# Moving all loads to one queue and fixing the start-up and tail order of an adaLN transformer block

## The chip, the cores and the metric

The kernel runs on one core of a Trainium2 chip (trn2). The metric is the device time of one execution in microseconds (us); where several executions were timed, the median is given with the lowest and highest. The names of the engines are those of the profile: PE does matmuls and transposes, DVE is VectorE, ACT is ScalarE, POOL is GpSimd, SP is SyncE. "PEclk" is the clock granted to PE, as a share of full speed.

## The reference

One transformer block on 2048 tokens of width D = 448. The vector `c` is turned into six modulation vectors. Each of the two halves of the block is a layernorm whose result is scaled and shifted by two of them, and whose output is multiplied by a third.

```python
mod = (silu(c) @ w_mod).reshape(1, 6, 1, -1)
sa, ca, ga, sb, cb, gb = mod[:, 0], mod[:, 1], ...          # cut
h = layernorm(x) * (1 + ca) + sa
x = x + ga * attention(h, wqkv, wo)      # 16 heads of 28, window of 8 tokens at distance 2
h = layernorm(x) * (1 + cb) + sb
x = x + gb * (silu(h @ w1) @ w2)         # hidden width 1792
```

## The kernel before

Tokens are split into even and odd ones, so that a window of 8 at distance 2 becomes 8 neighbours. There are six token groups (k = 0 to 5). The modulation is folded into the weights: `w_pad` is `wqkv` with its rows times `1 + ca`, `bq` is `sa @ wqkv` as a bias, `w1` is scaled by `1 + cb`, `wo` and `w2` by `ga` and `gb`.

The start-up has to produce, in this order of dependence: `scT` (silu of c, turned to a column), `modc_bf` (one modulation vector as columns, sixteen little matmuls into `ps_c`), `onep` (one plus it), twelve pieces of `w_pad`, `ps_b` and `bq`, and four rounds of layernorm on four token tiles each (statistics on DVE, power on POOL, `nmr` on DVE, `xn` on ACT, transpose on PE, copy to `h1T` on DVE). The order of the instructions on each engine is chosen by the framework's scheduler, except where the source adds an `after(later, earlier)`.

```python
# loads: three issuing engines
nc.sync.dma_start(out=x_all[:, 0:4, :], ...)
nc.scalar.dma_start(out=c_row[:], in_=c[0:1, :])
nc.scalar.dma_start(out=wmod_sb[:, 0:3, 0:2 * D], ...)
...                                                     # cut
nc.gpsimd.dma_start(out=wqkv_st[:, 0:3, :], ...)
nc.sync.dma_start(out=x_all[:, 4:8, :], ...)
nc.gpsimd.dma_start(out=wmod_sb[:, 0:3, 2 * D:6 * D], ...)
...                                                     # cut
# zero fills of the weights, all on POOL
nc.gpsimd.memset(wmod_sb[64:128, 3, :], 0.0)
nc.gpsimd.memset(wqkv_st[64:128, 3, :], 0.0)
nc.gpsimd.memset(w_pad[64:128, 3], 0.0)
nc.gpsimd.memset(w_pad[:].rearrange(...)[:, :, DH:32], 0.0)
...                                                     # cut: silu, ps_c, onep
for kt in range(NKT):
    for typ in range(3):
        nc.vector.tensor_scalar(out=w_pad[...], in0=wqkv_st[...], scalar1=onep[...], op0=ALU.mult)
...                                                     # cut: ps_b, bq
for q4 in range(1, 4):                                  # layernorm of groups of four tiles 1 to 3
    v_, a_ = layernorm_T([4 * q4 + i for i in range(4)], h1T, e_of_u, "a", use_pe=True)
    after(v_[0], bq_ins, "startup: critical vector-engine work first")
    ...
# the main loop
for k in range(NGRP + 1):
    if k < NGRP:
        attn_S(k, qkv_cur); pes = [attn_phase1(k, g, qkv_cur) for g in range(NG)]
    if k >= 1:
        post_a(UT_OF_GROUP[k - 1])      # ps_o, layernorm, DMA transposes into h2T
    if k < NGRP:
        attn_V(k, qkv_cur)
        for g in range(NG): attn_phase2(k, g, pes[g])
    if k + 1 < NGRP:
        qkv_next = project(k + 1)       # ps_p, evicted by ACT as "qkv"
    if k >= 1:
        post_b(prev, hid)               # ps_h, silu on ACT
        post_c(prev, hid)               # ps_y, output
```

## Time and profile before

| kernel before | us |
|---|---|
| time, 4 runs | 273.92 (272.8 to 274.78) |
| time of all its runs when the changed kernel was measured, those 4 included, 16 runs | 274.71 (272.8 to 276.0) |
| span of the profiled execution | 272.7 |
| first "qkv" eviction (end of start-up) | 57.51 |
| last group (from 237.2) | 35.5 |

The first lines of the profile's page for the kernel before: the busy time and share of each engine, then PE's busy tenths and its granted clock in 40 equal slices of the span (6.8 us each), and the load rate.

```profile
PE 206.4 (76%) x1902; PEld 130.8 (48%) x1902; DVE 154.3 (57%) x366; ACT 165.8 (61%) x292; POOL 33.1 (12%) x56
...
PE   0035635979799299988999889998994399914993
...
PEclk9999999999999779999999999999999579995999
...
GB/s 248 346 346 357 35 0 0 4 0 2 0 2 1 38 2 19 17 40 20 2 35 17 42 19 2 34 20 38 2 17 19 59 0 2 34 33 41 0 19 34
```

No engine is full. PE does nothing in the first two slices, is busy about half of the time or less in most of the next five, and is nearly empty again in the two slices "14" near the end (238.6 to 252.2 us). The next fence is the timeline of DVE in the start-up of the kernel before (start, busy time, engine, line, operation, and in brackets how long the engine sat idle before it and what ended the wait).

```profile
14.75 1.68 DVE L148 BATCH_NORM_STATS2 statsa<-x_all 128x6 f32<-128x448 bf16 x3 [7.50 <-DMA x_all<-in_A_x_dram]
16.35 0.14 DVE L154 SCALAR_TENSOR_TENSOR nmra<-mva,rstda 128x4 f32<-128x4 f32 x1
...
21.56 0.17 DVE L214 TENSOR_SCALAR onep_bf<-modc_bf 128x4 bf16<-128x4 bf16 x1
...
22.47 3.04 DVE L222 TENSOR_SCALAR w_pad<-wqkv_st,onep 128x448 bf16<-128x448 bf16 x12
...
31.09 0.17 DVE L238 COPY bq<-ps_q 128x12 f32<-128x12 f32 x1 [0.98 <-PE ps_q L237]
```

DVE takes its instructions in the order that it was given. The scheduler put statistics of the second x block ahead of the first `nmr`, and so DVE sat 7.5 us on a load, until 14.75, with nothing else done. `bq` comes at 31.09; three rounds of `nmr` follow at 33.9, 40.0 and 45.7 us, in lines left out here. The third view is PE's timeline in the last stretch of the kernel before.

```profile
217.35 11.30 PE L401 MATMUL ps_h<-h2T,w_sb 128*128 128x384 bf16 x56 [1.65 <-DMA h2T<-xn]
228.49 2.81 PE L410 MATMUL ps_y<-w_sb,hid 128*128 128x448 bf16 x14
...
239.65 0.35 PE L391 MATMUL ps_o<-x_all,ident 128*128 128x448 bf16 x1
248.93 10.88 PE L401 MATMUL ps_h<-h2T,w_sb 128*128 128x384 bf16 x56 [8.93 <-DMA h2T<-xn]
259.64 2.81 PE L410 MATMUL ps_y<-w_sb,hid 128*128 128x448 bf16 x14
```

The second half of the block for the last group cannot start until its layernorm and its DMA transposes are through: PE idles 8.9 us ahead of the last `ps_h`, with three short `ps_o` before that.

### The profile page before, as it was taken

The page shows a single profiled execution, that of the slowest core. Times are in us where ns is not written, and L with a number is a line of the kernel's source. Part 1 is how long each engine was busy: PE and PEld are TensorE (multiplying, and loading weights), DVE is VectorE, ACT ScalarE, POOL GpSimd, SP SyncE. Part 2 cuts the span into 40 slices and gives each one's busy share as a digit, 9 for nine tenths or more (in the row PEclk, how much of TensorE's full clock was granted, in tenths as well). Part 3 has the DMA queues.
Part 4 walks back from the last instruction along what each step waited for, and adds up shares of the span by engine and source line. Part 5 has one row for each costly group of instructions (what it writes and reads, how often), then busy time and mean ns, then how long its engine had stood idle before and what let it go on. Part 6 is the DMA issues. An engine that isn't in the chain of part 4 may idle for free.

```text
span 272.7 us, 4747 instructions
## 1 busy us (share of the span) xinstructions
PE 206.4 (76%) x1902; PEld 130.8 (48%) x1902; DVE 154.3 (57%) x366; ACT 165.8 (61%) x292; POOL 33.1 (12%) x56
## 2 busy tenths in 40 slices
PE   0035635979799299988999889998994399914993
PEld 0025623546466185655556555566852255502651
DVE  4056384579999995989209892099968500040000
ACT  2054076698768573899718996289944666241830
POOL 4890111000000000010010100101011000210001
PEclk9999999999999779999999999999999579995999
DMA  7999100000000100031010200001000200012000
GB/s 248 346 346 357 35 0 0 4 0 2 0 2 1 38 2 19 17 40 20 2 35 17 42 19 2 34 20 38 2 17 19 59 0 2 34 33 41 0 19 34
DMA packets 15392, 13.30 MB, mean 49 GB/s; under 512 B 9225, under 2 KB 13962, under 8 KB 15370
## 3 DMA queue, kind: packets, MB, share of 16 engines
q1 hardware_dynamic: 11296, 5.54, 8.1%
q0 software_dynamic: 1280, 4.65, 4.8%
q10 hardware_dynamic: 2794, 2.81, 3.4%
q8 instruction: 15, 0.25, 0.4%
q14 instruction: 7, 0.06, 0.1%
HBM read 9.06 MB, written 1.84 MB: 40 GB/s over the span
## 4 chain that ended last, share of the span: by engine, by line
PE 43%; DVE 25%; issue 13%; DMA 8%; ACT 6%; POOL 3%; SPq 0%; POOLq 0%; ACTq 0%
PE ps_h L401 15%; PE ps_y L410 13%; DMA x_all<-in_A_x_dram 5%; DVE mx L347 4%; DVE xm L349 3%; PE ps_p L324 3%; DMA h2T<-xn 3%; PE pst L165 2%; PE O L378 2%; DVE rs L369 2%; DVE statsb L148 2%; DVE statsa L148 2%; DVE pn L372 2%; ACT w_sb L261 2%; DVE S L336 2%
## 5 line engine op out<-in xcount | busy, mean ns | idle before, releaser
L401 PE MATMUL ps_h<-h2T,w_sb 128*128 128x384 bf16 (+1 forms) x336 | 56.7, 329 | 18.3 <-DMA h2T<-xn 17.5
L403 ACT ACTIVATE hid<-ps_h,b 128x384 bf16<-128x384 f32 (+1 forms) x84 | 44.3, 548 | 16.0 <-PE ps_h L401 13.0
L401 PEld LDWEIGHTS <-w_sb 128*128 128x128 bf16 x336 | 33.8, 103 | 38.1 <-issue 23.8
L324 PE MATMUL ps_p<-h1T,w_pad 128*128 128x344 bf16 (+1 forms) x288 | 47.7, 313 | 1.8 <-ACT qkv L326 1.7
L410 PE MATMUL ps_y<-w_sb,hid 128*128 128x448 bf16 x224 | 45.0, 352 | 0.0
L326 ACT ACTIVATE qkv<-ps_p,bq 128x344 bf16<-128x344 f32 (+1 forms) x72 | 35.6, 562 | 3.3 <-PE ps_p L324 3.0
L324 PEld LDWEIGHTS <-w_pad 128*128 128x128 bf16 x288 | 27.8, 98 | 17.7 <-issue 3.7
L410 PEld LDWEIGHTS <-hid 128*128 128x128 bf16 x224 | 21.9, 98 | 19.9
L347 DVE TENSOR_REDUCE mx<-L 128x14 f32<-128x448 f32 (+1 forms) x24 | 14.0, 621 | 28.2 <-PE L L345 28.2
L414 ACT CAST ot<-ps_y 128x448 bf16<-128x448 f32 x16 | 8.5, 532 | 34.9 <-PE ps_y L412 34.9
L159 ACT ACTIVATE xn<-x_all,nmra,rstda 128x448 bf16<-128x448 bf16 x16 | 10.8, 748 | 26.5 <-DVE nmra L154 24.3
L165 PE MATMUL pst<-ident,xn 128*128 128x128 bf16 x64 | 9.4, 309 | 22.8 <-ACT xn L159 21.7
L415 POOL DMA_DIRECT2D out_dram<-ot x16 | 9.0, 561 | 139.6 <-ACT ot L414 139.6
L148 DVE BATCH_NORM_STATS2 statsb<-x_all 128x6 f32<-128x448 bf16 x16 | 9.5, 610 | 23.8 <-ACT x_all L392 23.6
L378 PE MATMUL O<-pT,V 128*128 128x32 bf16 x344 | 12.6, 179 | 10.4 <-DVE pT L375 10.4
L165 PEld LDWEIGHTS <-xn 128*128 128x128 bf16 x64 | 6.0, 135 | 29.7 <-ACT xn L159 28.6
L378 PEld LDWEIGHTS <-V 128*128 128x128 bf16 x344 | 11.8, 98 | 13.3 <-issue 9.5
L336 DVE COPY S<-qkv 32x1792 bf16<-32x1792 bf16 (+1 forms) x24 | 14.9, 622 | 1.6 <-ACT qkv L326 1.3
L148 DVE BATCH_NORM_STATS2 statsa<-x_all 128x6 f32<-128x448 bf16 x16 | 9.4, 611 | 10.6 <-DMA x_all<-in_A_x_dram 10.6
L363 DVE COPY V<-vs 32x1792 bf16<-32x1792 bf16 (+1 forms) x24 | 15.1, 628 | 0.6
L390 PE MATMUL ps_o<-wo_pad,oT 128*128 128x448 bf16 x64 | 15.4, 352 | 0.0
L369 DVE TENSOR_REDUCE rs<-pe 128x14 f32<-128x448 f32 (+1 forms) x24 | 14.1, 602 | 1.2 <-ACT pe L352 1.1
(89 smaller groups left out, 264.6 us busy)
## 6 DMA issues: line engine op xcount, KB each, us to landing
x_all<-in_A_x_dram SPq DMA_DIRECT2D x4, 448.0 KB, 11.6
out_dram<-ot POOLq DMA_DIRECT2D x16, 112.0 KB, 2.0
w_sb<-in_B_w_dram ACTq DMA_DIRECT2D x1, 1568.0 KB, 25.5
wmod_sb<-in_w_mod_dram POOLq DMA_DIRECT2D x1, 1344.0 KB, 13.4
w_sb<-in_B_w_dram SPq DMA_DIRECT2D x1, 1344.0 KB
wqkv_st<-in_A_wqkv_dram POOLq DMA_DIRECT2D x1, 1008.0 KB, 9.3
wmod_sb<-in_w_mod_dram ACTq DMA_DIRECT2D x1, 672.0 KB
wo_pad<-in_A_wo_dram ACTq DMA_DIRECT2D x4, 98.0 KB
```

What stands on the lines that cost most here:

```text
L148: vops.append(nc.vector.bn_stats(out=stats[:, j, :], in_=x_all[:, U, :]))
L165: nc.tensor.transpose(pst[:, kt, :], xn[:, 128 * kt:128 * kt + 128], ident[:])
L324: nc.tensor.matmul(ps[:, 0:wd], lhsT=w_pad[:, kt, typ, g, :], rhs=h1T[:, kt, e0:e0 + wd], start=(kt == 0), stop=(kt == NKT - 1))
L326: nc.scalar.activation(out=tiles[typ][:, g, 0:wd], in_=ps[:, 0:wd], func=ACTF.Identity, bias=bq[:, typ * 4 + g:typ * 4 + g + 1])
L336: nc.vector.tensor_copy(out=_ap4(S4[:, 0, 0, :], 32 * hq, 32 * hq, ((TMAX * 128, NG), (128, T), (1, BW))), in_=_ap4(qg[:, 0, :], 32 * hq, ...
L347: nc.vector.tensor_reduce(out=mx[:, 0:T], in_=L[:, 0:T, :], axis=AX.X, op=ALU.max)
L369: nc.vector.tensor_reduce(out=rs[:, 0:T], in_=pe[:, 0:T, :], axis=AX.X, op=ALU.add)
L378: nc.tensor.matmul(O[:, j, :], lhsT=V4[:, g, j, :], rhs=pT[:, j, :], start=True, stop=True)
L390: nc.tensor.matmul(ps[:, 0:D], lhsT=oT[:, g, n0:n0 + 128], rhs=wo_pad[:, g, :], start=(g == 0), stop=False)
L401: nc.tensor.matmul(ps[:, 0:n], lhsT=w1_sb[:, kt, f * 128:(f + 1) * 128], rhs=h2T[:, kt, c0:c0 + n], start=(kt == 0), stop=(kt == NKT - 1))
L403: ins = nc.scalar.activation(out=hid[:, f, 0:n], in_=ps[:, 0:n], func=ACTF.Silu, bias=b1[:, f:f + 1])
L410: nc.tensor.matmul(ps[:, 0:D], lhsT=hid[:, f, j * 128:(j + 1) * 128], rhs=w2_sb[:, f, :], start=(f == 0), stop=False)
```

## The change

Its intent is to shorten the start-up and the tail. It has three parts. First, all loads go to the sync engine's queue, in order of need. Second, the instructions of the start-up are chained, so that each engine issues them in program order: the modulation matmuls come ahead of the first transposes, four of the twelve `w_pad` pieces go to ACT, and the statistics of the second x block come behind `bq` and the masks. Third, `post_a` of the last group moves from the round after the last to the end of the last round, ahead of `post_b` of the group before it. Along with the second part, the zero fill of `wo_pad` moves from POOL to DVE, and the fills of two small constants from DVE to POOL.

```diff
-    nc.scalar.dma_start(out=c_row[:], in_=c[0:1, :])
-    nc.scalar.dma_start(out=wmod_sb[:, 0:3, 0:2 * D], ...)
+    nc.sync.dma_start(out=c_row[:], in_=c[0:1, :])
+    nc.sync.dma_start(out=wmod_sb[:, 0:3, 0:2 * D], ...)
...                        # cut: all other loads likewise; wo, w1 and w2 follow at once
+    chains = {"v": [], "a": [], "p": []}
+    def V(ins):            # A, P and G (POOL) alike
+        chains["v"].append(ins)
+        return ins
...
+    mv0, rstd0 = ln_stats([0, 1, 2, 3], "a", wrap=V, wg=G)
+    A(nc.scalar.activation(out=sc_row[:, 0:D], in_=c_row[:], func=ACTF.Silu))
...                        # cut: scT, nmr0
+    G(nc.gpsimd.memset(wmod_sb[64:128, 3, :], 0.0))
+    mod_cols(1, 1, V, P)
+    make_onep(0, 1, V)
+    ev0 = ln_apply([0, 1, 2, 3], mv0, rstd0, h1T, e_of_u, "a", use_pe=True, ...)
...
+    G(nc.gpsimd.memset(wqkv_st[64:128, 3, :], 0.0))
+    G(nc.gpsimd.memset(w_pad[64:128, 3], 0.0))
+    G(nc.gpsimd.memset(w_pad[:].rearrange(...)[:, :, DH:32], 0.0))
...
+            if typ == 2:
+                A(nc.scalar.activation(out=o_, in_=i_, func=ACTF.Identity, scale=onep[0:rn, 0, kt:kt + 1]))
+            else:
+                V(nc.vector.tensor_scalar(out=o_, in0=i_, scalar1=onep[0:rn, 0, kt:kt + 1], ...))
+    mod_cols(0, 0, V, P)
...                        # cut: ps_b, b_unp, bq, masks
+    mv1, rstd1 = ln_stats([4, 5, 6, 7], "a", wrap=V)
+    ev1 = ln_apply([4, 5, 6, 7], mv1, rstd1, h1T, e_of_u, "a", use_pe=True, wv=V, wa=A)
...
+    w1_zero = nc.gpsimd.memset(w1_sb[64:128, 3, :], 0.0)
+    for name in ("v", "a", "p", "g"):
+        for x0, x1 in zip(chains[name], chains[name][1:]):
+            after(x1, x0, "start-up issue order")
...
-        if k >= 1:
+        if 1 <= k < NGRP:
             post_a(UT_OF_GROUP[k - 1])
...
+        if last:
+            post_a(UT_OF_GROUP[k])
         if k + 1 < NGRP:
             qkv_next = project(k + 1)
```

## The prediction

> **What bounds it now.** No engine is full (page, part 1: PE 76%, ACT 61%, DVE 57% of 272.7 us). The timeline has three stretches. (a) 0 to 57.6 us, start-up: a serial chain; PE is busy 25 of 57.6 us. (b) 57.6 to 237.2: PE busy 159 of 180 us. (c) 237.2 to 272.7, the last token group: PE does 2.8 us of ps_o, then waits for layernorm and DMA transposes. ps_h resumes at 248.9 (idle of 8.9 us, released by DMA h2T).
>
> **What the change does.**
> 1. All loads go to the sync queue, in order of need. Bytes are unchanged (9.06 MB read, about 350 GB/s while loading). The Trainium skill, "DMA: Bandwidth & Descriptors", section "Issuing engines are not separate DMA queues", says all issuers share the same 16 engines, so I expect no bandwidth lost or won. An estimate at 346 GB/s: c and the first w_mod columns by about 7 us, w_qkv by 10, everything by 29. None of these should be what waits longest. In before the second x block landed at 14.7 us, and the in-order DVE sat 7.5 us on it, which delayed the first nmr from about 8.5 to 16.4.
> 2. Chained order. The modulation matmuls go ahead of the first transposes, v's part of w_pad goes to ACT (DVE 12 to 8 pieces, 3.04 to 2.0 us), group-1 statistics come after bq. My sum: rstd 7.1, pow 1.04, POOL memset of w_mod 2.33 to about 10.7 (the new gate), ps_c 0.8, onep 12.2, four h1T copies to 13.8, w_pad to 15.8, ps_b 4.3, then 1.4 to bq: about 22 us against 31.26. Part is given back: masks, then three layernorm rounds run nearly serially (statistics 2.4, pow 1.0, four xn 2.7, transpose and copy 1). Before overlapped them more (nmr at 33.9, 40.0, 45.7); I expect 27.3, 35.8, 41.0. Then as before ps_b1 and the w1 scaling (6.83) stand on ACT ahead of the first qkv eviction. First qkv at about 52.5 against 57.5: gain about 5 us.
> 3. post_a of the last group moves ahead of post_b of group 4. Its layernorm and transposes then run under 20 us of PE work, so the 11.8 us between ps_y and ps_h go. Paid back: three ps_o hold three of four PSUM buffers, and ACT's order becomes x_all copies, table load, one hid, three xn (2.06, after nmr), thirteen hid. I expect PE to stall about 2.5 us early in ps_h of group 4 and post_c(4) to start 4 us later than 228.5. Net about 7.7 us.
>
> Stretch (b) keeps its instruction order, so it only shifts.
>
> **Sum.** 273.9 - 5 - 7.7 = about 261 us; 257.5 to 264.5 eight times in ten. Faster by over 2%: 0.96; within 2%: 0.03; slower: 0.01.
>
> **What would show it.** bq copy at 21 to 24 us; first qkv at 51 to 54; DVE not waiting for x at 7 to 15 us; load rate still about 350 GB/s; no PE gap over 2 us between the last ps_y of group 4 and the last ps_h; a new ACT-caused PE stall of 2 to 4 us in ps_h of group 4.
>
> **What would make it wrong.** One queue feeding the engines more slowly, so that w_mod lands after 11 us or w1 after 44; POOL set-up delaying eps or the memsets; DVE and POOL slowing each other at 11 to 17 us; layernorm rounds more or less serial than I summed (2 us either way); the group-5 x_all copies stalling ps_h longer than 4 us.

## The result

| | before | changed |
|---|---|---|
| time, median (lowest to highest) | 274.71 (272.8 to 276.0), 16 runs | 264.66 (263.58 to 266.15), 11 runs |
| ratio | | 0.9637 [0.9608, 0.9667] |
| span of the profiled execution | 272.7 | 262.2 |
| `bq` on DVE | 31.09 | 24.49 |
| `nmr` of the three later rounds | 33.90, 39.95, 45.73 | 30.31, 38.43, 43.77 |
| first qkv eviction | 57.51 | 55.55 |
| start of the S copies of the last group | 190.53 | 189.64 |
| `ps_h` of group 4 starts | 217.35 | 216.47 |
| from there to the end | 55.35 | 45.73 |

A ratio in this document is the mean time of one kernel's fast runs over the mean of the other's fast runs of the same rounds, so it is not quite the ratio of the medians that stand beside it. The brackets hold the 95% interval.

The change made the kernel faster by 3.6%, but it missed the predicted 261.0 us by 3.7 us and came to lie just above the range of 257.5 to 264.5. The page of the changed kernel has the same lines:

```profile
PE 207.6 (79%) x1902; PEld 130.9 (50%) x1902; DVE 157.2 (60%) x361; ACT 167.2 (64%) x296; POOL 28.7 (11%) x53
...
PE   0337425989889479998999969999899657799993
...
PEclk9999999999979959999999999999999959799999
...
GB/s 228 356 328 294 180 0 0 4 0 2 0 0 2 21 23 0 38 0 63 0 2 54 2 60 0 2 35 21 41 2 18 20 60 0 61 2 51 2 20 35
```

The end of the start-up is ACT's first "qkv" eviction, here first in the kernel before, then in the changed one:

```profile
57.51 4.48 ACT L326 ACTIVATE qkv<-ps_p,bq 128x368 bf16<-128x368 f32 x9
```

```profile
55.55 6.35 ACT L370 ACTIVATE qkv<-ps_p,bq 128x368 bf16<-128x368 f32 x12
```

In the page, the slices are now 6.6 us. The end of PE's row has no empty slice any more ("99657799993" where before "4399914993" stood). The start is only a little fuller. There is a new weak place in the clock row, the 7 three places ahead of the first 5 (72 to 79 us). The load rate of the first slices is about as before (228, 356, 328 and 294 against 248, 346, 346 and 357), and a rest is carried in the fifth slice.

DVE in the start-up of the changed kernel:

```profile
12.31 1.46 DVE L245 TENSOR_SCALAR onep_bf<-modc_bf 128x4 bf16<-128x4 bf16 x1
...
15.31 3.61 DVE L272 TENSOR_SCALAR w_pad<-wqkv_st,onep 128x448 bf16<-128x448 bf16 x8
...
24.49 0.17 DVE L285 COPY bq<-ps_q 128x12 f32<-128x12 f32 x1 [0.69 <-PE ps_q L284]
```

The 7.5 us wait for x is gone, as predicted. Two things were not expected. The little `onep_bf` on 128x4 elements took 1.46 us, where the kernel before needed 0.17. And eight pieces of `w_pad` took 3.61 us, where twelve had taken 3.04. What POOL did at that time is in its own timeline:

```profile
11.21 1.21 POOL L260 MEMSET wqkv_st<- 64x1344 bf16 x1
12.37 1.37 POOL L261 MEMSET w_pad<- 64x1536 bf16 x1
...
16.21 1.60 POOL L307 MEMSET w_sb<- 64x1792 bf16 x1
```

POOL's memset of `w_pad` ran from 12.37 to 13.74, and the 1.46 us of `onep_bf` end at 13.77. One of the eight `w_pad` pieces took 1.74 us where the median is 0.33: it started at 16.21, the next one at 17.87, and POOL's memset of `w_sb` ran from 16.21 to 17.81. Copies from PSUM on DVE at the same time (four `h1T` copies, 1.52 us in all) were not lengthened. The Trainium skill has this in "SBUF — State Buffer", section "Who interferes with whom": DVE and POOL share one pair of ports, a copy, cast or `tensor_scalar` in a 2-port mode takes it for the whole instruction, as does a POOL instruction, and the one that comes second "fully blocks". The numbers fit that, and they fit with no sharing: the DVE instructions ended with the memsets. Which of the two came second is not clear from the starts: `onep_bf` started 0.06 us ahead of the memset that it ended with, while the memset before that one (11.21 to 12.42) still ran.

The third place is the end. PE's timeline of the last stretch of the changed kernel:

```profile
216.47 0.90 PE L445 MATMUL ps_h<-h2T,w_sb 128*128 128x384 bf16 x3 [0.60 <-DMA h2T<-xn]
...
221.13 0.81 PE L445 MATMUL ps_h<-h2T,w_sb 128*128 128x384 bf16 x4 [0.52 <-ACT hid L447]
224.38 7.40 PE L445 MATMUL ps_h<-h2T,w_sb 128*128 128x384 bf16 x36 [2.44 <-ACT hid L447]
231.62 2.81 PE L454 MATMUL ps_y<-w_sb,hid 128*128 128x448 bf16 x14
...
240.14 9.26 PE L445 MATMUL ps_h<-h2T,w_sb 128*128 128x384 bf16 x56
249.24 2.81 PE L454 MATMUL ps_y<-w_sb,hid 128*128 128x448 bf16 x14
```

The last `ps_h` follows straight on the last `ps_y` of group 4, at 240.14. What was paid for it is seen in the idle times of 0.52 and 2.44 us behind "ACT hid". And the last fifty-six `ps_h` take 249.24 - 240.14 = 9.10 us from start to start of the next group, where before they took 259.64 - 248.93 = 10.71.

The account of the profiled executions is then: start-up -2.0 us (57.51 to 55.55), the middle +1.1 (the lead at `ps_h` of group 4 is only 217.35 - 216.47 = 0.9), the tail -9.6 (55.35 to 45.73). The sum is -10.5, which is 272.7 less 262.2. The prediction had -5, 0 and -7.7.

Three questions follow. Was the tail's gain really that large, and apart from the rest? Why did the start-up give 2 us and not 5? And where did 1.1 us go in the middle, where no instruction was moved? (One caution on the 2 us: in another execution with the same start-up as the kernel before, the tail run below, the second x block let go 0.7 us sooner and the first qkv came at 56.80; in two more with the changed start-up it came at 55.33 and 55.44. The gain of the start-up is thus 1.3 to 2.2 us, by the pair of profiles.)

### The profile page after: what moved, and what is told of

Read it like the earlier page. It is cut to its first block, busy times and chain, and to the rows that moved or that the text cites. A ratio compares the mean times of both kernels' runs of the same rounds, so it can differ in the third digit from the quotient of the medians.

```text
span 262.2 us, 4748 instructions
## 1 busy us (share of the span) xinstructions
PE 207.6 (79%) x1902; PEld 130.9 (50%) x1902; DVE 157.2 (60%) x361; ACT 167.2 (64%) x296; POOL 28.7 (11%) x53
## 3 DMA queue, kind: packets, MB, share of 16 engines
q0 software_dynamic: 768, 1.84, 2.0%
HBM read 9.06 MB, written 1.84 MB: 42 GB/s over the span
## 4 chain that ended last, share of the span: by engine, by line
PE 35%; DVE 26%; issue 18%; ACT 10%; POOL 4%; DMA 4%; POOLq 0%; SPq 0%; ACTq 0%; DVEq 0%
PE ps_h L445 12%; PE ps_y L454 10%; DVE mx L391 4%; DVE xm L393 3%; DMA h2T<-xn 3%; DVE statsb L180 3%; ACT xn L202 3%; PE ps_p L368 3%; DVE rs L413 2%; ACT qkv L370 2%; PE pst L208 2%; ACT w_sb L333 2%; PE O L422 2%; DVE S L380 2%; PE ps_b L278 2%
## 5 line engine op out<-in xcount | busy, mean ns | idle before, releaser
L445 PE MATMUL ps_h<-h2T,w_sb 128*128 128x384 bf16 (+1 forms) x336 | 54.8, 321 | 10.9 <-DMA h2T<-xn 6.8
L368 PE MATMUL ps_p<-h1T,w_pad 128*128 128x344 bf16 (+1 forms) x288 | 49.0, 319 | 1.3 <-ACT qkv L370 1.2
L447 ACT ACTIVATE hid<-ps_h,b 128x384 bf16<-128x384 f32 (+1 forms) x84 | 43.7, 548 | 7.2 <-PE ps_h L445 4.3
L445 PEld LDWEIGHTS <-w_sb 128*128 128x128 bf16 x336 | 33.0, 101 | 29.3 <-issue 14.2
L434 PE MATMUL ps_o<-wo_pad,oT 128*128 128x448 bf16 x64 | 17.6, 387 | 0.6 <-ACT oT L424 0.6
L419 DVE STREAM_TRANSPOSE pT<-pn 128x448 bf16<-128x448 bf16 (+1 forms) x24 | 14.6, 634 | 0.1
L416 DVE TENSOR_TENSOR pn<-pe,rs 128x448 bf16<-128x448 f32 (+1 forms) x24 | 14.3, 624 | 0.1
L405 DVE STREAM_TRANSPOSE vs<-qkv 128x448 bf16<-128x448 bf16 (+1 forms) x24 | 14.2, 631 | 0.2
```

Of the source, the lines that this page charges most:

```text
L368: nc.tensor.matmul(ps[:, 0:wd], lhsT=w_pad[:, kt, typ, g, :], rhs=h1T[:, kt, e0:e0 + wd], start=(kt == 0), stop=(kt == NKT - 1))
L434: nc.tensor.matmul(ps[:, 0:D], lhsT=oT[:, g, n0:n0 + 128], rhs=wo_pad[:, g, :], start=(g == 0), stop=False)
L445: nc.tensor.matmul(ps[:, 0:n], lhsT=w1_sb[:, kt, f * 128:(f + 1) * 128], rhs=h2T[:, kt, c0:c0 + n], start=(kt == 0), stop=(kt == NKT - 1))
L447: ins = nc.scalar.activation(out=hid[:, f, 0:n], in_=ps[:, 0:n], func=ACTF.Silu, bias=b1[:, f:f + 1])
```

## The experiments

Each run was timed against the kernel before in the same rounds on the same chip. The medians of before in the three lots of runs were 275.29, 274.8 and 274.8 us (11 runs each). In the second lot (the first test of the old queues, the queue move alone, and the two kernels under "Putting it together") one run of before came in at 270.96. Runs over 1.5% above the fastest count as slow and stay out of the ratios, so this one run shuts out five of the other ten; it widens the intervals of the second lot and raises its ratios by about 0.3%, and the record's verdict for all four kernels of the lot is "unclear".

### The tail alone, and the start-up alone

The first theory is that the two parts add: the tail is worth some 9.5 us and the start-up some 2. The rival is that the tail is worth what was predicted and the start-up carries more than its 2 us. The first kernel is before, with the third part of the change alone.

```diff
@@ on the kernel before
-        if k >= 1:
+        if 1 <= k < NGRP:
             post_a(UT_OF_GROUP[k - 1])
...
+        if last:                     # k == NGRP - 1
+            post_a(UT_OF_GROUP[k])
```

> The kernel before with part 3 alone (post_a of the last group ahead of post_b of group 4). Theory A (read from the two traces: tail worth 9.6 us of the 10.5, because the 11.8 us gap goes, about 4 us are paid back in ps_h of group 4, and the last ps_h also runs about 1.6 us faster since PE no longer restarts at a low granted clock after an idle of 9 us): about 9.5 us faster than before, ratio 0.965. My recorded sum: 7.7 us, ratio 0.972. The last ps_h should take about 9.2 us in theory A against 10.9 before.

Measured: 265.03 us (264.12 to 266.58), ratio 0.9643 [0.9596, 0.9691]. The last `ps_h` took 9.1 us from 240.41.

The second kernel is the changed one with the tail put back.

```diff
@@ on the changed kernel
-        if 1 <= k < NGRP:
+        if k >= 1:
             post_a(UT_OF_GROUP[k - 1])
...
-        if last:
-            post_a(UT_OF_GROUP[k])
```

> The changed kernel with the last post_a back at its old place: start-up rework and queue move alone. Theory A: 1 to 2 us faster than before (first qkv at 55.5 against 57.5), ratio 0.993 to 0.997; the last ps_h again takes about 10.7 us at a granted clock under 1. Recorded sum: 5 us faster, ratio 0.982.

Measured: 272.95 us (271.91 to 273.62), ratio 0.9917 [0.9866, 0.9968]; first qkv at 55.33; the last `ps_h` takes 10.7 us again. The tail is worth about 10 us on its own and the start-up about 2. With the old start-up and with the new one, the last `ps_h` is fast if and only if the gap ahead of it is gone: 9.1 us after no wait, 10.7 after the 9 us idle. The granted clock over the last `ps_h` is 0.84 in the kernel before (0.50 in its first 2 us, 1.00 from 253.0 on) and 0.85 with the start-up alone; it is 1.00 in the changed kernel and with the tail alone. The Trainium skill says in "TensorE: Matmul & The Clock Gate", section "What's actually happening", that the clock is halved after an idle window of about 3.4 us and given back after a busy one of that length; the slower restart agrees with it.

Added up, the two medians would give 275.29 - 10.3 - 2.3 = 262.7 us for both parts, 2 us less than the changed kernel took. The intervals are about 1.3 us wide to each side, so this alone shows nothing, but it is on the side of something lost in the middle; "The middle" below settles most of it.

### POOL's zero fills out of the way of DVE

The theory is that POOL's memsets held DVE in the start-up. Here the memsets of `w_pad` and `w1` move ahead of POOL's first power, to 1.6 to 6.1 us, when DVE clears tiles, waits for x and then runs statistics.

```diff
@@ on the changed kernel
+    G(nc.gpsimd.memset(w_pad[64:128, 3], 0.0))
+    G(nc.gpsimd.memset(w_pad[:].rearrange(...)[:, :, DH:32], 0.0))
+    G(nc.gpsimd.memset(w1_sb[64:128, 3, :], 0.0))
     mv0, rstd0 = ln_stats([0, 1, 2, 3], "a", wrap=V, wg=G)
...
-    G(nc.gpsimd.memset(w_pad[64:128, 3], 0.0))
-    G(nc.gpsimd.memset(w_pad[:].rearrange(...)[:, :, DH:32], 0.0))
...
-    w1_zero = nc.gpsimd.memset(w1_sb[64:128, 3, :], 0.0)
```

> The changed kernel with three POOL memsets (two on w_pad, one on w1) moved into POOL's idle time before its first pow (2.7 to 7.8 us). Theory A (DVE's SBUF-to-SBUF bf16 instructions wait for a running POOL memset: onep_bf took 1.46 us and one w_pad piece 1.74 us in after, against 0.15 and 0.33): both fall to their usual time, bq at about 21.7 us instead of 24.5, first qkv at about 52.7 instead of 55.6, total about 2.8 us under the changed kernel, ratio to before about 0.953. Rival (those two instructions are long for another reason, such as waiting for a weight load to land): unchanged, bq at 24.5, ratio 0.963.

Measured: 261.79 us (260.26 to 262.76), ratio 0.9515 [0.9464, 0.9566]. DVE in this run:

```profile
12.28 0.17 DVE L248 TENSOR_SCALAR onep_bf<-modc_bf 128x4 bf16<-128x4 bf16 x1
...
14.19 2.04 DVE L273 TENSOR_SCALAR w_pad<-wqkv_st,onep 128x448 bf16<-128x448 bf16 x8
...
21.81 0.17 DVE L286 COPY bq<-ps_q 128x12 f32<-128x12 f32 x1 [0.69 <-PE ps_q L285]
```

`onep_bf` is back to 0.17 us, the eight pieces to 2.04, and `bq` comes 2.7 us sooner. The later rounds of `nmr` are at 27.62, 35.74 and 41.08, the first qkv at 52.87. The prediction had 27.3, 35.8, 41.0 and 52.5. So with this one collision taken out, the start-up is what the prediction had summed.

An earlier memset could also help in another way, say because `w_pad` is ready sooner. So the next kernel keeps the early memsets and adds three of the same sizes at the old place, onto a scratch tile that nothing reads.

```diff
@@ on the kernel of the last experiment
     G(nc.gpsimd.memset(wqkv_st[64:128, 3, :], 0.0))
+    scratch = const.tile([128, 2688], BF16, name="scratch")
+    G(nc.gpsimd.memset(scratch[64:128, 0:1536], 0.0))
+    G(nc.gpsimd.memset(scratch[:, 0:2688].rearrange("p (x d) -> p x d", d=14)[:, :, 0:4], 0.0))
+    G(nc.gpsimd.memset(scratch[64:128, 0:1792], 0.0))
```

> e3 plus three POOL memsets of the same sizes as those moved, on a scratch tile that nothing reads, at the place the moved ones had. Theory A: the two long DVE instructions come back, bq at 24 to 24.5 us, ratio to before about 0.963 again. Rival (moving helped because w_pad and w1 were ready earlier, a matter of data and not of POOL being busy): as fast as e3, 0.953.

Measured: 263.98 us (262.92 to 265.14), ratio 0.9603 [0.9554, 0.9651]; first qkv at 55.51. First DVE, then POOL in this run:

```profile
12.22 1.45 DVE L248 TENSOR_SCALAR onep_bf<-modc_bf 128x4 bf16<-128x4 bf16 x1
...
15.22 3.65 DVE L277 TENSOR_SCALAR w_pad<-wqkv_st,onep 128x448 bf16<-128x448 bf16 x8
...
24.43 0.17 DVE L290 COPY bq<-ps_q 128x12 f32<-128x12 f32 x1 [0.69 <-PE ps_q L289]
```

```profile
12.27 1.37 POOL L265 MEMSET scratch<- 64x1536 bf16 x1
...
16.64 1.60 POOL L267 MEMSET scratch<- 64x1792 bf16 x1
```

The stalls are back to within 0.04 us, though no instruction reads what these memsets write. A dependence is excluded. The six times (262.92 to 265.14 us) and the six of the run before (260.26 to 262.76) do not overlap. So 2.6 of the 3 us that the start-up fell short were DVE held while POOL filled; that the shared port is the reason is the page's account, which no run here tests apart.

### The queues apart from the order

The prediction gave the queue move no worth in bandwidth. The first test puts the loads of the changed kernel back on the old queues, in the old order, with the wo and w2 issues on ACT.

```diff
@@ on the changed kernel
-    nc.sync.dma_start(out=c_row[:], in_=c[0:1, :])
+    nc.scalar.dma_start(out=c_row[:], in_=c[0:1, :])
...                        # likewise all loads, as in the kernel before
-        nc.sync.dma_start(out=wo_pad[32 * hq:32 * hq + DH, :, :], in_=wo_v[hq])
+        nc.scalar.dma_start(out=wo_pad[32 * hq:32 * hq + DH, :, :], in_=wo_v[hq])
```

> The changed kernel with the loads issued as before (c, w_mod head, wo and w2 from ACT, w_qkv and the rest of w_mod from POOL, x and w1 from sync); order of the engines as changed. My reading: in the changed order no instruction waits for the later loads (group-1 statistics start at 25.8 us, x block 2 landed long before), so the queue move is worth little here: within 1 us of the changed kernel, ratio to before 0.960 to 0.968. Rival (the queue move is the gain of the start-up): first qkv back at 57 us or later, ratio about 0.971.

Measured: 269.64 us (266.27 to 271.52), ratio 0.9828 [0.9739, 0.9916], unclear as a verdict, and 5 us worse than expected. ACT's timeline in this run ("ACTq" is the issue of a DMA):

```profile
2.35 12.38 ACTq L131 DMA_DIRECT2D wo_pad<-in_A_wo_dram  x4
...
15.22 1.28 ACT L224 ACT_TABLE_LOAD   x1 [15.22 <-DMA wo_pad<-in_A_wo_dram]
16.51 0.57 ACT L224 ACTIVATE sc_row<-c_row 1x448 bf16<-1x448 bf16 x1
```

The expectation missed because the test was badly built. The four wo issues stood ahead of silu on ACT; from the first to the last of them ACT did nothing else, from 2.35 to 14.73. Each took 0.3 to 0.6 us; the time lies between them, as the third started at 8.17 and the fourth at 14.41. In the compiled program each of the last three, and the w2 issue, waits for a semaphore of an earlier load; the traces show the gaps and not what was waited for. So silu ran at 16.51 where the changed kernel has it near 4.1, `bq` came at 29.08 and the first qkv at 60.14. The loads themselves were not slow. The test was mended later: the same queues, but the wo and w2 issues stand on ACT behind its `w_pad` pieces.

```diff
@@ on the kernel of the last experiment
-    for hq in range(4):
-        nc.scalar.dma_start(out=wo_pad[...], in_=wo_v[hq])       # ahead of everything
-    nc.scalar.dma_start(out=w2_sb[:], ...)
...
+    for hq in range(4):
+        A(nc.scalar.dma_start(out=wo_pad[...], in_=wo_v[hq]))    # behind w_pad
+    A(nc.scalar.dma_start(out=w2_sb[:], ...))
     mod_cols(0, 0, V, P)
```

> The full change with all loads on the old queues again, but this time the four wo issues and the w2 issue stand on ACT behind the last piece of w_pad, so that ACT has nothing to wait for ahead of silu. Theory (the queue itself carries no time; the 5 us of the first old-queue run came from ACT held at 2.4 to 14.8 us by a DMA issue that waits): silu starts at about 4 us as in the full change, bq at 22 to 26 us, first qkv eviction within 2 us of 55.6, time within 2 us of 264.7, ratio to before .957 to .970. Rival (the old queues themselves bring the loads later): first qkv still at 59 us or later, time 268 to 271.

Measured: 265.13 us (264.33 to 266.53), ratio 0.9664 [0.9621, 0.9707]; silu at 3.63, `bq` at 24.62, first qkv at 55.70. ACT in this run:

```profile
3.63 0.57 ACT L221 ACTIVATE sc_row<-c_row 1x448 bf16<-1x448 bf16 x1
```

This is the changed kernel's time within half a us. In the chained kernel the queue is therefore worth nothing in itself that these runs could tell from noise. The Trainium skill, in "DMA: Bandwidth & Descriptors", section "Issuing engines are not separate DMA queues", says the same of the transfers; it adds that issuing from several engines only saves sequencer time, "which is usually small relative to the DMA itself". The time of an issue on ACT is indeed small here (0.3 to 0.9 us each in the two tests). But issues that have to wait, on an engine with work behind them, were not small: 12.4 us of ACT in the first of the two tests.

The next kernel is before, with the queue move alone.

```diff
@@ on the kernel before
-    nc.scalar.dma_start(out=c_row[:], in_=c[0:1, :])
+    nc.sync.dma_start(out=c_row[:], in_=c[0:1, :])
...                        # likewise all loads, in the order of the changed kernel
```

> The kernel before with the queue move alone. In before DVE waited 7.5 us for x block 2 ahead of the first nmr, which came at 16.4 us. My reading: with x block 2 later in one queue the scheduler now puts the first nmr ahead of that wait, so nmr at 8.5 to 9.5, bq some 5 us earlier than 31.3; the later chain keeps part of it: first qkv 2 to 5 us earlier than 57.5, ratio 0.982 to 0.993. Rival (queue choice changes nothing, all issuers share the same engines): ratio 1.000 within 0.004.

Measured: 268.97 us (267.9 to 270.74), ratio 0.9844 [0.978, 0.9907]. The ratio was within what was expected (just below it, 0.981, if the runs of before that the rule shuts out are kept), but the first qkv came at 50.08, 7.4 us sooner than before and 5.5 us sooner than in the fully changed kernel. The rounds of `nmr` in this run:

```profile
8.28 0.17 DVE L154 SCALAR_TENSOR_TENSOR nmra<-mva,rstda 128x4 f32<-128x4 f32 x1 [1.15 <-POOL rstda L152]
...
25.49 0.16 DVE L154 SCALAR_TENSOR_TENSOR nmra<-mva,rstda 128x4 f32<-128x4 f32 x1 [0.68 <-POOL rstda L152]
...
30.60 0.16 DVE L154 SCALAR_TENSOR_TENSOR nmra<-mva,rstda 128x4 f32<-128x4 f32 x1 [0.85 <-POOL rstda L152]
...
36.43 0.16 DVE L154 SCALAR_TENSOR_TENSOR nmra<-mva,rstda 128x4 f32<-128x4 f32 x1 [0.90 <-POOL rstda L152]
```

With the loads on one queue the scheduler no longer puts statistics of x block 2 ahead of the first `nmr`, which comes at 8.28 instead of 16.35. And it keeps running the statistics of later rounds in the holes of earlier ones, so the rounds are about 5 to 6 us apart; in the chained kernel the second and third are 8.1 us apart. POOL's fills (12.38 to 17.91) stretch DVE here too: the twelve `w_pad` pieces take 4.56 us instead of 3.04. Still `bq` comes at 21.66, so this is not what sets the two orders apart. Of the 7.4 us, 3 were lost again on the way in the profiled execution, at 270.32 us one of the slower of the six: the granted clock of the whole run is 0.936 against 0.956 of before, and its row has more weak slices in the first half. All six runs are low (0.936 to 0.949, against 0.95 to 0.956 of before in the same rounds).

So the chained order would be a loss at the first qkv. To see whether this holds at the end, the next kernel has the queue move and the tail, and not the chained order.

```diff
@@ on the kernel of the last experiment
-        if k >= 1:
+        if 1 <= k < NGRP:
             post_a(UT_OF_GROUP[k - 1])
...
+        if last:                     # k == NGRP - 1
+            post_a(UT_OF_GROUP[k])
```

> Before with the queue move and the moved post_a of the last group, without the chained issue order and without the split of w_pad to ACT. Theory (the chained order costs about 5 us against what the scheduler does once the x wait is gone): first qkv eviction at about 50 us instead of 55.6, tail about 9.5 us shorter than before, time 258 to 262, ratio .940 to .955, so faster than the full change. Rival (the first qkv time of the queue-only run does not carry to the end, its time is eaten by the granted clock or by waits in the attention): time 263 to 267, no faster than the full change.

Measured: 259.82 us (256.95 to 261.1), ratio 0.9428 [0.9374, 0.9481]; first qkv at 49.97. It is 4.8 us faster than the full change (timed in other rounds; against before, 0.9428 and 0.9637), with less of it. Then which part of the chained order costs this? The rounds point to the statistics of the second x block, which the chain holds until `bq` and the masks are through. One more kernel moves only these ahead of the copy of `b_unp`, into 4.6 us in which DVE idles for `ps_b`.

```diff
@@ on the changed kernel
+    mv1, rstd1 = ln_stats([4, 5, 6, 7], "a", wrap=V, wg=G)
+    nmr1 = ln_nmr([4, 5, 6, 7], mv1, rstd1, "a", V)
     b_unp = small.tile([128, 12], F32, name="b_unp")
...
-    mv1, rstd1 = ln_stats([4, 5, 6, 7], "a", wrap=V)
-    ev1 = ln_apply([4, 5, 6, 7], mv1, rstd1, ..., wv=V, wa=A)
+    ev1 = ln_apply([4, 5, 6, 7], mv1, rstd1, ..., wv=V, wa=A, nmr=nmr1)
```

> The full change with one thing moved: the statistics, power and nmr of token group 1 stand ahead of the copy of b_unp in DVE's chain, where DVE idles 4.6 us on ps_b, instead of behind bq and the masks. Theory (the chained order makes the layernorm rounds serial behind bq, and that is what the start-up lost against the queue move alone): bq unchanged at 24 to 25 us, nmr rounds at about 24, 33 and 39 us instead of 30.3, 38.4, 43.8, first qkv at 50 to 52 us, time 260 to 262. Rival (other things gate the first qkv: the w1 load and scaling, or the clock): first qkv within 1 us of 55.6, time within 1 us of 264.7.

Measured: 257.57 us (255.81 to 259.58), ratio 0.9388 [0.9341, 0.9435]. This is lower than expected. DVE in this run:

```profile
15.27 2.19 DVE L272 TENSOR_SCALAR w_pad<-wqkv_st,onep 128x448 bf16<-128x448 bf16 x8
...
22.00 0.16 DVE L190 SCALAR_TENSOR_TENSOR nmra<-mva,rstda 128x4 f32<-128x4 f32 x1 [1.20 <-POOL rstda L184]
...
23.04 0.17 DVE L287 COPY bq<-ps_q 128x12 f32<-128x12 f32 x1 [0.69 <-PE ps_q L286]
...
37.27 0.16 DVE L190 SCALAR_TENSOR_TENSOR nmra<-mva,rstda 128x4 f32<-128x4 f32 x1 [1.05 <-POOL rstda L184]
```

All later rounds come 6.5 us or more sooner, and the first qkv at 49.06, 6.5 us sooner than in the changed kernel. `bq` was expected unchanged and came 1.45 us sooner. This was a side effect: the power of this round now stands in POOL's chain ahead of the `w1` memset, which therefore starts at 22.03 instead of 16.21 and no longer meets the `w_pad` pieces, which take 2.19 us instead of 3.61. So, by subtraction, 5.0 of the 6.5 us belong to the order of the statistics and 1.5 to the fill; the two were not run apart.

### The middle

The last question is the 1.1 us that the changed kernel lost between 57 and 203 us. There PE does the same work in the same order in both kernels. The lead at the S copies is 1.97 us twice and then 0.58; the loss falls between the second and the third group. In the profile of the changed kernel the granted clock is 0.50 from 73.8 to 77.0 us. The changed kernel was profiled once more, unaltered.

```diff
@@ on the changed kernel
(no edit)
```

> The full change unaltered, profiled a second time, to see whether the dip of the granted clock to 0.50 at 73.8 to 77.0 us, which took about 1.4 us of the lead of the start-up, belongs to the kernel. Theory (the dip comes with the stretch of work of this kernel and its alignment): a dip in the same slice again, and the S copy of the last group at 202 to 203 us. Rival (the dip falls differently from execution to execution): no dip near 75 us, and the last S copies start about 2 us ahead of before (201.3 us), span about 261.

Measured: 262.65 us, one run (its state is unknown, since one run alone cannot be placed), beside 274.88 of before; span 260.8. (The expectation's 201 to 203 us are not S copies but work some 13 us behind them; the last group's S copies are at 190.53 in before, 189.64 in the changed kernel and 188.35 here.) The two executions of one and the same kernel, with busy times and PEclk of two stretches (the columns are the stretch, its length, busy us and instructions of PE, PEld, DVE, ACT and POOL, the clock, and the share and rate of DMA). First the changed kernel, then its second profile:

```profile
70.20:73.60 3.40, 1.52 (x27) 1.04 (x26) 3.40 (x9) 1.58 (x5) 0.00 (x0) 1.00 0.00 0
73.80:77.00 3.20, 3.20 (x18) 1.53 (x15) 3.20 (x9) 0.69 (x3) 0.00 (x0) 0.50 0.00 0
```

```profile
70.20:73.60 3.40, 1.52 (x32) 1.08 (x30) 3.40 (x8) 1.58 (x4) 0.00 (x0) 1.00 0.00 0
73.80:77.00 3.20, 3.09 (x27) 1.76 (x25) 3.20 (x9) 1.65 (x5) 0.00 (x0) 1.00 0.00 0
```

In both, PE was busy 1.52 of 3.4 us ahead of the place. In the one the clock was then halved for 3 us, in the other it was not. With no dip, the lead of the S copies of the second run is 2.08 us for three groups and 2.18 at the last, so the whole lead of the start-up arrives. The middle's loss in the first profile is the clock's, and not one of order or of waits. The Trainium skill, "TensorE: Matmul & The Clock Gate", section "What's actually happening", calls the window free-running and its effect run-variable; this pair of runs agrees, with 1.4 us between them.

It is not pure chance either, it seems. The time from the S copies of the second group to those of the third is 19.44 us without the dip and 20.8 to 21.0 with it. In five profiles the first qkv falls between 55.3 and 55.7 us, and four of them have the dip (changed, start-up alone, scratch memsets, old queues mended). Of eight others with the first qkv elsewhere one has it there (queue move alone), and one more loses about 2.6 us one group earlier (queue move with tail, 22.1 us from the first to the second S copies against 19.5 in before). Why it should depend on the time of the start stays open: one profile of each kernel is too few.

The timed runs have no trace, but the record gives the mean clock of each. It comes in steps, and the times follow it. The changed kernel has 0.966 in one of twelve runs (263.58 us, the fastest), 0.961 in four (263.95 to 264.1), 0.959 in five (264.03 to 265.27) and 0.955 in two (265.9 and 266.15). The second profile, without the dip, had 0.966, and the first, with it, 0.959. So eleven of twelve runs lost more clock than the one without the dip, though a mean does not say where.

This also bears on the 2 us that were missing when the parts were added. The mean time of before at 0.956 was 273.7 us, and of the start-up alone at the same clock 272.2; the tail alone took 264.5 in its three runs at 0.966. Added up at these clocks the parts give 263.0. The changed kernel took 263.58 and 262.65 us at 0.966. One step lower (0.95 with the old tail, 0.959 with the new one) the sum is 263.9 and the changed kernel 264.8. At equal clock, then, the shortfall is under 1 us. The tail alone simply met the higher clock in three of six runs, the changed kernel in one of twelve.

### Putting it together

The two last kernels try to use what was found. The first bundles several edits of the start-up: the `wmod` and `wqkv` fills (and the masks') early on POOL, the other fills on ACT, the rest of `w_mod` loaded ahead of x blocks 3 and 4, the second modulation vector ahead of the transposes, and the statistics of the second x block ahead of `b_unp`.

```diff
@@ on the changed kernel
+    G(nc.gpsimd.memset(wmod_sb[64:128, 3, :], 0.0))      # ahead of the first power
+    G(nc.gpsimd.memset(wqkv_st[64:128, 3, :], 0.0))
...
     A(nc.scalar.activation(out=sc_row[:, 0:D], in_=c_row[:], func=ACTF.Silu))
+    A(nc.scalar.memzero(w_pad[64:128, 3]))
+    A(nc.scalar.memzero(w_pad[:].rearrange(...)[:, :, DH:32]))
+    A(nc.scalar.memzero(w1_sb[64:128, 3, :]))
...
     make_onep(0, 1, V)
+    mod_cols(0, 0, V, P)
...
+    mv1, rstd1 = ln_stats([4, 5, 6, 7], "a", wrap=V, wg=G)
+    nmr1 = ln_nmr([4, 5, 6, 7], mv1, rstd1, "a", V)
     b_unp = small.tile([128, 12], F32, name="b_unp")
```

> The changed kernel with e3 taken further: the POOL memsets that gate ps_c run before POOL's first pow, three zero fills go to idle ACT, group-1 statistics go into DVE's 4.6 us wait for ps_b. Sum of durations: ps_c at 7.8 instead of 11.3, bq at about 18, nmr of group 1 at about 18 instead of 30.3; then two more serial layernorm rounds of about 8 and 5.5 us as before and the w1 scaling: first qkv at about 43 against 55.6, total about 252 us, ratio about 0.92. If the layernorm rounds are limited by something else than DVE's order, first qkv later than 48.

Measured: 253.95 us (253.13 to 255.81), ratio 0.9292 [0.9234, 0.9349]; `bq` at 20.2, first qkv at 45.6, each some 2 us later than expected. The share of each edit was not measured, except for what the run with the early statistics shows.

The last kernel also takes work out of the start-up that the first group does not need: `project(0)` follows right on `bq`, and the layernorm of later tiles, the scaling of `w1`, `wo` and `w2` go into the attention of the first groups.

```diff
@@ on the kernel of the last experiment
-    late_setup_compute()                 # ahead of project(0)
...
+    ln1_apply()                          # behind project(0)
     for k in range(NGRP + 1):
...
+            if k == 0:
+                qkv_1 = project(1)
+                w1_setup()
...
+        if k == 0:
+            scale_rows(wo_pad[:], g_bc[0], NG)
+            ln_late(2)
+            qkv_next = qkv_1
...
+        if k == 2:
+            ln_late(3)
```

> e7 with project(0) issued directly after bq (it needs only layernorm group 0), and w1 scaling, wo and w2 scaling and the layernorm groups 1 to 3 moved into the attention of the first groups. If the start-up chain and not engine time is what costs, first qkv at 20 to 25 us and total 235 to 245 us, ratio 0.86 to 0.89. If the moved work only lengthens the middle (ACT and DVE there are 70% busy), the total stays near e7.

Measured: 243.23 us (242.62 to 245.58), ratio 0.8903 [0.8835, 0.8971], with a correct result (as all the runs had). It beats both kernels of the case. The first 56 us of the kernel before, then of this one (columns as above):

```profile
0.00:56.00 56.00, 24.86 (x262) 18.62 (x263) 27.81 (x106) 25.07 (x30) 18.94 (x34) 1.00 0.49 163
```

```profile
0.00:56.00 56.00, 38.22 (x456) 27.76 (x456) 45.42 (x131) 46.43 (x67) 10.21 (x27) 0.95 0.54 163
```

PE has 38.2 us of work in the first 56 us where before it had 24.9, and the first qkv eviction is at 26.7 us (20 to 25 were expected).

## Why the prediction was right or wrong

It was right that the change makes the kernel faster, and by more than 2%. It was wrong in the size: 261.0 was predicted, 264.66 measured.

- **"My sum: ... onep 12.2, four h1T copies to 13.8, w_pad to 15.8 ... about 22 us against 31.26."** This is the step that failed. It costed DVE's instructions with durations from the kernel before, where they ran at 21.6 to 25.5 us and POOL's fills were over; the change moves them to 12 to 18 us, under POOL's fills. `onep` was ready at 14.0, `w_pad` at 18.9, `bq` at 24.49. About 1.3 us went in `onep_bf` and 1.6 in `w_pad`. With the fills moved, the same sum held: `bq` 21.81, first qkv 52.87; with empty fills put back it failed again, at 24.43 and 55.51. The range was missed by 0.16 us, so this term alone was enough: with the fills moved the kernel took 261.79. The danger stood in the last paragraph ("DVE and POOL slowing each other at 11 to 17 us"), but no size was given to it and the range did not hold it.
- **"I expect 27.3, 35.8, 41.0 ... First qkv at about 52.5 against 57.5: gain about 5 us."** Missed by that same term, carried on: 30.3, 38.4, 43.8 and 55.55, a gain of 2.0. The spacing of the rounds was right.
- **What the parts of the start-up are worth.** The prediction saw that "part is given back" by the serial rounds, and sized it well (9.3 us gained at `bq`, 5 kept at the first qkv; measured 6.6 and 2.0). But it set the chain against the old order alone, and not against what the scheduler would do once the loads had moved. The queue move alone, which lets the scheduler do the first `nmr` ahead of x block 2, brought 7.4 us at the first qkv; the rest of the new start-up took 5.5 of these back. With the tail, the kernel without the chain took 259.82 us, the full change 264.66.
- **"All loads go to the sync queue ... no bandwidth lost or won."** Right: with the old queues and the same order on the engines, 265.13 us.
- **"Net about 7.7 us"** for the tail. The mechanism was right to the tenth: the gap went (from the start of `ps_y` of group 4 to the last `ps_h` it was 20.44 us and is 8.52, 11.9 less, where 11.8 had been put), PE stalled 2.96 us on ACT in `ps_h` of group 4, and `ps_y` came 4.0 us later counted from the start of that `ps_h`. The missing term was the last `ps_h` itself: 9.10 us instead of 10.71, since it no longer starts after a long idle. That makes 11.9 - 4.0 + 1.6 + 0.1 = 9.6.
- **"Stretch (b) keeps its instruction order, so it only shifts."** Right for the instructions; in the profiled run 1.1 us of the lead was lost to a lower granted clock, and in a second profile it was not.

The sum, from 261.0 up: start-up +3.0, tail -1.9, the middle +1.1, before itself 274.71 instead of 273.92 +0.8, the rounding of the predicted sum +0.2, and 0.45 because the profiled spans differ by 10.5 and the medians by 10.05. This gives 264.65. The errors of start-up and tail partly cancelled; without that the miss would have been larger. That the dip in the middle also falls in most of the timed runs fits their mean clocks (below 0.966 in eleven of twelve), which do not show the place.

## What to carry to other kernels

A duration read from a trace holds for the company it was read in: when a change moves an instruction to another time, look at what the other engines do at the new time, above all DVE against POOL's fills and memsets. When a change has several parts, price each against what the scheduler would do without it; here an explicit order, written to help, hid 5 us of gain that one of the other parts had brought. And an engine that computes should not have a DMA issue that waits ahead of its work.

## What the Trainium skill lacked or had wrong

- "SBUF — State Buffer": right and, in hindsight, the page that would have mended the prediction. The case that it measures in full is a DMA's; these runs add the size for plain DVE operations: a `tensor_scalar` on 128x4 bf16 went from 0.17 to 1.46 us beside a memset of 1.37 us, and one 64x448 piece of `w_pad` from 0.33 to 1.74 beside one of 1.60. They also show a point that the section does not treat: `onep_bf` had started 0.06 us ahead of the memset with which it ended, while the memset before it still ran, so two memsets in a row can both go ahead of it.
- "DMA: Bandwidth & Descriptors", section "Issuing engines are not separate DMA queues": right on bandwidth (265.13 against 264.66 us), but its remark that only a usually small issue time is at stake leaves out issues that have to wait: four of them held ACT for 12.38 us, and the kernel took 269.64 us.
- "TensorE: Matmul & The Clock Gate": gives an idle window of about 3.4 us. In these runs a stretch of 3.4 us in which PE was busy 1.52 us, with a longest idle of 1.84 us, was followed in one execution by a clock of 0.50 for 3 us and in another of the same kernel by 1.00. The page calls the number of slow matmuls at a kernel's start run-variable and says further down that short idles can make the clock swing in mid-kernel; it gives no length for such idles, and does not say that the same idle can bring the dip in one run and not in another.
